# Row block 3 of h turned on chip for the w2 gradient, and the other h loads put into spent gradient slots, in a one-core forward-and-backward block

## The chip, the cores and the metric

The kernel runs on one core of one Trainium2 chip. A core has five engines that run side by side, each with its own instruction stream: TensorE (PE) multiplies matrices, VectorE (DVE) and ScalarE (ACT) work elementwise, GpSimd (POOL) does little here, and SyncE (SP) issues most of the DMA transfers; ACT and POOL issue some as well. The metric is the device time of the whole program in microseconds (us), the median of several executions.

## The reference

The reference runs a block forward and then the gradient of all its inputs for a given grad_out. It has 2048 rows (S) of width D = 512, and an MLP of hidden width F = 1792.

```python
mod = silu(c) @ w_mod -> sa, ca, ga, sb, cb, gb
h = layernorm(x) * (1 + ca) + sa
x = x + ga * irfft2(rfft2(h) * (w_r + 1j * w_i))
h = layernorm(x) * (1 + cb) + sb
r = relu(h @ w1 + b1);  h = r * r
x = x + gb * (h @ w2 + b2)
_out, _vjp = jax.vjp(_f, A_x, A_w_r, A_w_i, B_w1, B_b1, B_w2, B_b2, c, w_mod)
```

There are ten outputs: x, and nine gradients. Two matter below: the gradient of w1 (512 x 1792), a product of the MLP's input with the inner gradient, and the gradient of w2 (1792 x 512), a product of the hidden activation h = r² with the incoming gradient. Both sum over all 2048 rows.

## The kernel before

The rows are cut into NT = 16 tiles of 128, and four tiles make a row block (NB = 4 blocks). F is cut into NFC = 14 chunks of 128 ("fc"). The Fourier transforms are matrix products with constant tables. In order of time the stages are: start, layernorm 1, the first transform and `back_products` (L892: the gradient of h, kept in `gall` with 14 slots for each row block); the spectral forward stage; the MLP stage, block by block; the w1 gradient beside the spectral backward stage; and the w2 gradient beside the last row pairs of the spectral backward stage.

**MLP stage.** For each block, `stage_h` forms h for two fc at a time: four matmuls for each fc (L1064), ReLU on ACT, the square on DVE into a tile of the ring `hring`, and the product of r with the inner gradient in place in `gall` (L1071, ACT sums over it in L1073). Here h lies with f on the partitions and rows along them. `stage_o` multiplies h by w2, `stage_gn` the inner gradient by w1T (L1096, `row_product`). `hring` holds seven pairs, one block. For the w2 gradient, h is needed with rows on the partitions: each pair is stored in DRAM (`h_dram`, L1074), and is turned when it is read back. The inner gradient is turned from SBUF to SBUF, two fc of a block at a time (`ghn_part`, L1049, a DMA transpose of 128x8x128), and overwrites its slot in `gall`. `Cdb` and `LFb` (L1223, L1228) are tables, `h_sb` (L1234, four loads) is the other operand of the w1 gradient; it takes the place of w1T, so its loads wait for the last read of w1T in `stage_gn`.

**w1 gradient.** `grad_w1` runs 16 units (L1342): the first eight read the fc 0 to 6 of all blocks of `gall`, the last eight the fc 7 to 13.

**w2 gradient.** `grad_w2` (L1441) runs 14 groups, one for each fc, of 16 matmuls 128x512 over the 16 row tiles. Chunks 10 and 13 are cut in halves of 256 columns; the order is 0 to 9, 10a, 11, 12, 10b, 13a, 13b. ACT copies each result (L1442), and SP stores it (L1443; ACT itself the last half). `load_hn` (L1252) brings one fc of h from `h_dram`, turned, in one DMA transpose of 128x16x128 on SP's queue:

```python
pool = hnp if fc < 2 else endp.get("hn", endp["gw"])
hns.append(pool.tile([P, NT, P], BF16, name="hn", bufs=2 if pool is not endp.get("hn") else 6))
nc.sync.dma_start(hns[fc], h_dram[fc, :, :], transpose=True)
...
while len(hns) < min(NFC, max(fc + 4, min(2 * fc + 6, 10))):
```

So fc 0 and 1 have a pool that exists early, fc 2 and 3 another pair, fc 4 to 9 six buffers in the pool `endp`, which takes the place of `gall` once all units of the w1 gradient are done, and fc 10 to 13 reuse the buffers of fc 4 to 7. The tail's work tiles (gs, gh1, q1, gw) lie in the same pool.

**Row pairs.** Beside the w2 gradient, for t = 0, 2, ..., 14, `row_pair` and `row_end` finish two row tiles of the gradient of x on DVE and ACT. Each needs two loaded tiles (n1 and gxl, `load_rows3`, L1333 and L1334, on SP); the loads for t + 6 stand after the end of t. Then `gm.emit` (L488 to L502) forms a part of the gradient of w_mod with weights loaded in L481 (`wmc`), and L1563 to L1570 the gradient of c.

**What sets the order.** `set_order` arranges each engine's instructions by a table of numbers, ORDER, written out for PE, ACT, DVE, POOL and SP. An engine takes its stream strictly in that order, and so does SP with the transfers it issues: one that waits for a buffer, or takes long to issue, holds up all that stand behind it.

## Time and profile before

| | |
|---|---|
| median of 3 runs | 396.31 us (394.63, 396.31, 396.81) |
| span of the profiled execution | 398.0 us |
| PE busy | 382.1 us, 96% |
| DVE busy | 334.8 us, 84% |
| ACT busy | 303.2 us, 76% |
| MLP stage, about | 103 to 258 us |
| w1 gradient (L1342), about | 259 to 328 us |
| w2 gradient (L1441), about | 331 to 393 us |

The profile is of one execution, on the hardware. The span runs from its first to its last recorded event; it is the profiled execution's own time. A line of the timeline gives start and duration in us, the engine, the line of the code, the operation, "output<-input", a count, and in brackets the idle time before it and what ended that. SPq is SP issuing a transfer; its duration is the time for which SP is held by that issue, not the time of the transfer. "DMA to landing" is the time from the start of the issue to the arrival of the data. PEclk is the clock that TensorE was granted, 1.00 being full. Buffer names are those of the tiles, with a slot number (hn_1s is slot 1 of `hn`). "Waits" name an engine's instruction, what it waited for, the total time in us, the number of times and the longest.

### The profile page before, as it was taken

Reading aid. Unit: us, or ns where it says so; the run is one execution under the profiler, and the core shown is the slowest. Engines: PE = TensorE matmul, PEld = TensorE weight load, DVE = VectorE, ACT = ScalarE, POOL = GpSimd, SP = SyncE. Lnnn points to the kernel's source line nnn. Section 1 sums busy time; section 2 is a strip of 40 time slices with the busy share of each in tenths; the row PEclk is TensorE's granted clock in tenths of the full one; section 3 lists DMA queues with packets and bytes.
Section 4 is the critical chain, followed back from the end, with each engine's and each line's share of the span. In section 5 each row is a group of like instructions: output and inputs, shape, how many; then the busy total and the mean of one; then the engine's idle time right before and its main releaser. Section 6 shows DMA issues by size and latency. Waiting matters only on the chain.

```text
span 398.0 us, 8415 instructions
## 1 busy us (share of the span) xinstructions
PE 382.1 (96%) x3042; PEld 202.4 (51%) x3042; DVE 334.8 (84%) x822; ACT 303.2 (76%) x605; POOL 33.3 (8%) x114
## 2 busy tenths in 40 slices
PE   8999999999999999999999999999999999999495
PEld 3555677544444444444444435457666664444244
DVE  8899959949986699969997999957999989998430
ACT  4787899899896499759976999277665589998441
POOL 9151001000000000000000000012300000002100
PEclk9999999999999999999999999999999999999979
DMA  8999799874589999578928696999979998999995
GB/s 258 362 222 293 230 209 252 209 280 63 195 228 197 256 259 253 128 191 183 257 81 210 167 245 180 270 245 371 296 221 262 215 325 173 221 208 243 249 259 189
DMA packets 133957, 91.06 MB, mean 229 GB/s; under 512 B 86842, under 2 KB 119868, under 8 KB 133660
## 3 DMA queue, kind: packets, MB, share of 16 engines
q1 hardware_dynamic: 132904, 88.09, 87.1%
q0 software_dynamic: 832, 2.36, 1.8%
q8 instruction: 24, 0.39, 0.4%
q14 instruction: 17, 0.14, 0.1%
q10 hardware_dynamic: 180, 0.07, 0.1%
HBM read 38.70 MB, written 33.19 MB: 181 GB/s over the span
## 4 chain that ended last, share of the span: by engine, by line
PE 74%; ACT 12%; DMA 5%; DVE 4%; POOL 2%; issue 1%; SPq 0%; ACTq 0%; POOLq 0%; DVEq 0%
PE og_1s L1096 12%; PE og_0s L1096 11%; PE mm_0s L1441 6%; PE mm_1s L1441 6%; PE mm_0s L1342 5%; PE mm_1s L1342 5%; PE mm_1s L1064 4%; PE mm_0s L1064 4%; PE pst L1064 3%; DMA hn_1s<-h_dram 3%; PE mm_0s L892 2%; DMA Xb<-xs_dram 2%; ACT AE L359 2%; PE mm_1s L892 2%; ACT gab L896 2%; ACT gab L1073 1%
## 5 line engine op out<-in xcount | busy, mean ns | idle before, releaser
L1342 PEld LDWEIGHTS <-h_sb 128*64 128x64 bf16 (+1 forms) x464 | 28.7, 109 | 15.9 <-issue 0.9
L1073 ACT ACTIVATE gab<-gab 128x512 bf16<-128x512 bf16 x56 | 35.0, 648 | 0.5 <-DVE gab L1071 0.5
L1096 PEld LDWEIGHTS <-gab 128*128 128x128 bf16 x224 | 21.5, 98 | 27.0 <-ACT gab L1073 1.9
L1064 PEld LDWEIGHTS <-w 128*128 128x128 bf16 x224 | 21.2, 98 | 25.7 <-issue 1.7
L1342 PE MATMUL mm_0s<-gab,h_sb 128*64 128x384 bf16 (+2 forms) x288 | 32.7, 345 | 0.0
L892 PEld LDWEIGHTS <-w2T 128*128 128x128 bf16 (+1 forms) x280 | 22.9, 102 | 18.5 <-issue 3.9
L1096 PE MATMUL og_0s<-w1T,gab 128*128 128x512 bf16 x112 | 27.4, 379 | 0.2 <-ACT G_0s L1109 0.2
L1096 PE MATMUL og_1s<-w1T,gab 128*128 128x512 bf16 x112 | 27.6, 379 | 0.0
L1441 PE MATMUL mm_0s<-g_sb,hn_1s 128*128 128x512 bf16 x64 | 16.8, 423 | 6.0 <-DMA hn_1s<-h_dram 6.0
L1342 PE MATMUL mm_1s<-gab,h_sb 128*64 128x512 bf16 (+2 forms) x176 | 22.4, 370 | 0.0
L1064 PE MATMUL mm_1s<-h2T,w 128*128 128x512 bf16 x84 | 21.9, 379 | 0.0
L1064 PE MATMUL mm_0s<-h2T,w 128*128 128x512 bf16 x80 | 21.2, 379 | 0.0
L359 ACT ACTIVATE AE<-psB 128x1024 bf16<-128x1024 f32 x16 | 17.2, 1078 | 0.7 <-PE psB L355 0.6
L896 ACT CAST gab<-mm_1s 128x512 bf16<-128x512 f32 x24 | 14.8, 615 | 2.3 <-PE mm_1s L892 2.2
L892 PE MATMUL mm_0s<-gT_0s,w2T 128*64 128x512 bf16 (+1 forms) x76 | 16.1, 380 | 0.2 <-DVE gab L894 0.2
L892 PE MATMUL mm_1s<-gT_0s,w2T 128*128 128x512 bf16 (+1 forms) x72 | 15.6, 379 | 0.1
L1064 PE MATMUL pst<-h2T,w 128*128 128x512 bf16 x60 | 15.6, 379 | 0.0
L892 PE MATMUL mm_1s<-gT_1s,w2T 128*128 128x512 bf16 (+1 forms) x68 | 14.9, 379 | 0.3 <-ACT gab L896 0.2
L892 PE MATMUL mm_0s<-gT_1s,w2T 128*128 128x512 bf16 (+1 forms) x64 | 15.1, 379 | 0.0
L1441 PEld LDWEIGHTS <-hn_1s 128*128 128x128 bf16 x64 | 6.8, 107 | 15.3 <-DMA hn_1s<-h_dram 6.2
L321 POOL MEMSET AE<- 128x4 bf16 x4 | 0.4, 110 | 162.4 <-PE mm_1s L1064 162.4
L1441 PE MATMUL mm_1s<-g_sb,hn_0s 128*128 128x512 bf16 (+1 forms) x64 | 13.7, 352 | 0.0
(650 smaller groups left out, 1064.3 us busy)
## 6 DMA issues: line engine op xcount, KB each, us to landing
w<-in_B_w_dram SPq DMA_DIRECT2D x2, 1792.0 KB, 10.4
Xb<-xs_dram SPq DMA_DIRECT2D x4, 514.0 KB, 7.9
Z<-wz_dram SPq DMA_DIRECT2D x4, 514.0 KB, 7.5
x_sb<-in_A_x_dram SPq DMA_DIRECT2D x4, 512.0 KB, 6.2
n_dram<-x_sb SPq DMA_DIRECT2D x4, 512.0 KB, 6.2
h_dram<-h2r SPq DMA_DIRECT2D x8, 256.0 KB, 2.4
h_sb<-h_dram SPq DMA_DIRECT2D x4, 512.0 KB, 5.4
g_sb<-in_grad_out_dram SPq DMA_DIRECT2D x2, 1024.0 KB
```

The costliest lines, as they stand in the source:

```text
L321: nc.gpsimd.memset(ae[:, :, :, 256:257], 0.0)
L359: nc.scalar.activation(dst, ps.rearrange("p r b (e f) -> p (r b) f e", e=2), AF.Copy, scale=EF_S)
L892: nc.tensor.matmul(ps[m], lhsT=w2T[:, dc, fc * P + m.start:fc * P + m.stop], rhs=gT[b][:, :, dc, :], start=(dc == 0), stop=(dc == 3), **pos)
L896: nc.scalar.copy(out=gaT[b][:, fc, :], in_=ps)
L1064: nc.tensor.matmul(ps, lhsT=w1[:, dc, (fc + i) * P:(fc + i + 1) * P], rhs=h2T[b][:, :, dc, :], start=(dc == 0), stop=(dc == 3))
L1073: nc.scalar.activation(gh[:, i, :], gh[:, i, :], AF.Copy, accum_out=gb1[:, b, fc + i:fc + i + 1])
L1096: nc.tensor.matmul(ps, lhsT=lhs(fc), rhs=rhs[:, fc, :], start=(fc == 0), stop=(fc == NFC - 1))
L1342: nc.tensor.matmul(blocks(ps[m], fb), lhsT=h2_sb[:, t, dc * P + m.start:dc * P + m.stop], rhs=gh_rows(t, fb), start=(t == 0), stop=(t == N ...
L1441: nc.tensor.matmul(ps[:, 0:w], lhsT=hns[fc][:, t, :], rhs=g_sb[:, t, c:c + w], start=(t == 0), stop=(t == NT - 1))
```

## The change

1. The h tiles of row block 3 (the last) are not stored in `h_dram`, which shrinks to 12 row tiles. They stay in `hring`, and seven DMA transposes of 128x8x128 (L1243 of the new code) turn them from SBUF to SBUF into a new tile `hr`, on SP's queue during `stage_gn(3)`.
2. `load_hn` (L1287 of the new code) brings 12 row tiles, as 128x12x128, into spent slots of `gall`: fc goes to slots 14·(fc mod 4) + 3·(fc div 4 mod 2) and the two after it. That gives eight places, which are free once the first eight units of the w1 gradient have read them. Four loads stand at the point where two stood, four more where two more stood, and then one for each group; fc 8 to 13 reuse the places of fc 0 to 5. The group of fc reads `hr` for its last four row tiles (`h_rows`).
3. The tail's tiles gs, gh1, q1, gw come from `gall` as well (`place`, `Ring`), so `gall` is held to the end.
4. A pool `early` takes some tiles of `rows` (r, h2r, h2T, and n2rows of the even blocks). It is released before `Cdb` is loaded; that load now waits for the last reads and writes of these tiles.
5. ORDER is replaced for all five engines. The number of PE's rows is the same.

The diff, with most of the table cut:

```diff
...
     "SP": (
-        "3 1 0 2 4 6 5 8 7 38 24 9 20 22 12 25 27 29 28 21 26 30 55 10 23 11 13 33 31 36 32 35 34 37 14-15 39 16-18 40 47 44 41 "
...
+        "3 1 0 2 4 6 5 8 7 23 12 9 11 10 32 36 31 13 34 14 28-29 20-21 37 27 119 22 25 35 30 33 24 17 16 38 15 26 18 44 125 52 47 "
...
-    h_dram = dram.tile([NFC, P, NT * P], BF16, name="h_dram")
+    h_dram = dram.tile([NFC, P, (NT - TB) * P], BF16, name="h_dram")
...
+    early = Slots(tc, name="early", bufs=1)
...
-                    n2b[b] = rows.tile([P, TB, D], BF16, name="n2rows")
+                    n2b[b] = (rows if b % 2 else early).tile([P, TB, D], BF16, name="n2rows", bufs=1)
...
-                r = rows.tile([P, 2, SB], BF16, name="r")
+                r = early.tile([P, 2, SB], BF16, name="r", bufs=2)
...
-                nc.sync.dma_start(h_dram[fc:fc + 2, :, sl].rearrange("a p s -> p a s"), h2)
+                if b < NB - 1:
+                    nc.sync.dma_start(h_dram[fc:fc + 2, :, sl].rearrange("a p s -> p a s"), h2)
+                else:
+                    hpair[fc] = h2
...
+                early.release()
                 w1p.release()
                 cdp = Slots(tc, name="cdp", bufs=1, side="right")
                 K["Cd"] = cdp.tile([P, D], BF16, name="Cdb")
...
-                merge(stage_gn(b, UT), [x for p in zip(again, parts + [lambda: None]) for x in p])
+                hrp = Slots(tc, name="hrp", bufs=1, side="right")
+                hr = hrp.tile([P, NFC, TB, P], BF16, name="hr")
+                turns = [lambda fc=fc: nc.sync.dma_start(hr[:, fc:fc + 2].rearrange("p a j c -> p (a j) c"), hpair[fc].rearrange("p a s -> p (a s)"), transpose=True)
+                         for fc in range(0, NFC, 2)]
+                merge(stage_gn(b, UT), [x for p in zip(again, parts + [lambda: None], turns + [lambda: None]) for x in p])
...
+    spare = [NFC * b + 6 for b in range(NB)] + [NFC * b + k for b in range(NB) for k in range(7, NFC)] + [NB * NFC, NB * NFC + 1]
...
         if fc < NFC:
-            pool = hnp if fc < 2 else endp.get("hn", endp["gw"])
-            hns.append(pool.tile([P, NT, P], BF16, name="hn", bufs=2 if pool is not endp.get("hn") else 6))
+            a = NFC * (fc % 4) + 3 * (fc // 4 % 2)
+            hns.append(gall[:, a:a + 3, :].rearrange("p a (j c) -> p (a j) c", c=P))
             nc.sync.dma_start(hns[fc], h_dram[fc, :, :], transpose=True)
+
+    def h_rows(fc, t):
+        return hns[fc][:, t, :] if t < NT - TB else hr[:, fc, t - (NT - TB), :]
...
-                load_hn()
-                load_hn()
+                for _ in range(4):
+                    load_hn()
...
-                nc.tensor.matmul(ps[:, 0:w], lhsT=hns[fc][:, t, :], rhs=g_sb[:, t, c:c + w], start=(t == 0), stop=(t == NT - 1))
+                nc.tensor.matmul(ps[:, 0:w], lhsT=h_rows(fc, t), rhs=g_sb[:, t, c:c + w], start=(t == 0), stop=(t == NT - 1))
...
-        while len(hns) < min(NFC, max(fc + 4, min(2 * fc + 6, 10))):
+        while len(hns) < min(NFC, fc + 9):
             load_hn()
...
-    for _ in range(2):
+    for _ in range(4):
         load_hn()
...
-                    gap.release()
-                    endp["hn"] = endp["gm"] = Slots(tc, name="endp", bufs=2)
+                    endp["gs"], endp["gh1"], endp["q1"], endp["gw8"] = Ring(2, 6), Ring(2, 3), Ring(2, 3), Ring(1, 8)
...
-            gs = (endp["gm"].tile([P, 2, D], BF16, name="gs", bufs=6) if "gm" in endp and t >= 6 else fp.tile([P, 2, D], BF16, name="gs", bufs=3))
+            gs = (endp["gs"].tile() if "gs" in endp and t >= 6 else fp.tile([P, 2, D], BF16, name="gs", bufs=3))
...
```

**Place 1: SP's queue at the end of the MLP stage, before.** h_dram<-h are stores of h of block 3, gab<-gab the transposes of the inner gradient of blocks 2 and 3 (`gab` is the name of `gall`), gx_dram<-n2rows stores of row results.

```order
L1223 DMA Cdb<-Cd_dram 128x512
L1074 DMA h_dram<-h_4s 128x2x512
L1228 DMA LFb_3510<-LF_dram 128x1024
L1228 DMA LFb_3509<-LF_dram 128x1024
L1049 DMA_TRANSPOSE gab<-gab 128x8x128
L1074 DMA h_dram<-h_6s 128x2x512
L1074 DMA h_dram<-h_5s 128x2x512
L1049 DMA_TRANSPOSE gab<-gab 128x8x128 x2
L1134 DMA gx_dram<-n2rows_1s 128x1024
L1234 DMA h_sb<-h_dram 128x2048 x2
L1049 DMA_TRANSPOSE gab<-gab 128x8x128
L1234 DMA h_sb<-h_dram 128x2048 x2
```

The same place in the new program:

```order
L1235 DMA Cdb<-Cd_dram 128x512
L1243 DMA_TRANSPOSE hr<-h_2s 128x8x128
L1243 DMA_TRANSPOSE hr<-h_4s 128x8x128
L1243 DMA_TRANSPOSE hr<-h_1s 128x8x128
L1243 DMA_TRANSPOSE hr<-h_3s 128x8x128
L1243 DMA_TRANSPOSE hr<-h_5s 128x8x128
L1240 DMA LFb_3506<-LF_dram 128x1024
L1057 DMA_TRANSPOSE gab<-gab 128x8x128
L1250 DMA h_sb<-h_dram 128x2048
L1145 DMA gx_dram<-n2rows 128x1024
L1250 DMA h_sb<-h_dram 128x2048
L1057 DMA_TRANSPOSE gab<-gab 128x8x128
```

The stores of h are gone, and five of the seven new transposes stand between `Cdb` and the first load of `h_sb`. The other two follow the third load of `h_sb`, and one load of `h_sb` comes after them.

**Place 2: SP's queue at the start of the row pairs, before.** hn<-h_dram are reloads of h, n_0s and n_1s the n1 tiles of row pairs t = 0, 6, 12 and t = 2, 8, 14, out_dram<-Xb stores of another gradient.

```order
L1257 DMA_TRANSPOSE hn_5s<-h_dram 128x16x128
L1349 DMA out_dram<-gw_1s 128x896
L1402 DMA out_dram<-Xb 32x4x257
L1257 DMA_TRANSPOSE hn_0s<-h_dram 128x16x128
L1402 DMA out_dram<-Xb 32x4x257
L1257 DMA_TRANSPOSE hn_1s<-h_dram 128x16x128
L1334 DMA gxl_0s<-gx_dram 128x1024
L1333 DMA n_0s<-n_dram 128x1024
```

In the new program (n_5089 is the n1 tile of t = 4, the n_0s here that of t = 6, which waits for the end of row pair 0):

```order
L1287 DMA_TRANSPOSE gab<-h_dram 128x12x128
L1382 DMA out_dram<-gw_1s 128x896
L1367 DMA gxl<-gx_dram 128x1024
L1366 DMA n_0s<-n_dram 128x1024
L1366 DMA n_5089<-n_dram 128x1024
L1287 DMA_TRANSPOSE gab<-h_dram 128x12x128
L1432 DMA out_dram<-Xb 32x2x1028
L1367 DMA gxl_1s<-gx_dram 128x1024
```

These are the seventh and the eighth reload of the new program; in the old one hn_5s is the fourth. The n1 load of t = 4 stood 15 rows further up before; it now stands behind that of t = 6.

**Place 3: SP's queue in the last third of the w2 gradient, before.** out_dram<-gw are stores of finished groups.

```order
L481 DMA wmc_0s<-in_w_mod_dram 128x4x512
L1443 DMA out_dram<-gw_1s 128x512
L1257 DMA_TRANSPOSE hn_0s<-h_dram 128x16x128
L1334 DMA gxl_1s<-gx_dram 128x1024
L1257 DMA_TRANSPOSE hn_1s<-h_dram 128x16x128
L1443 DMA out_dram<-gw_2s 128x512
L1257 DMA_TRANSPOSE hn_2s<-h_dram 128x16x128
L481 DMA wmc_1s<-in_w_mod_dram 128x4x512
L1257 DMA_TRANSPOSE hn_3s<-h_dram 128x16x128
```

The last reloads of the new program:

```order
L481 DMA wmc_0s<-in_w_mod_dram 128x4x512
L1476 DMA out_dram<-gab 128x512 x3
L1287 DMA_TRANSPOSE gab<-h_dram 128x12x128 x2
L1367 DMA gxl_0s<-gx_dram 128x1024
L1476 DMA out_dram<-gab 128x512
L1367 DMA gxl_1s<-gx_dram 128x1024
```

Before, four reloads stand behind the store of the group that hn_0s waits on, and 18 stores come after the last of them. Now two reloads (fc 12 and 13) stand behind the stores of the first six groups, and both `wmc` loads are ahead of them. On PE, the transpose of `gcb` (L1567; L1599 in the new code) was the last instruction of all and now stands ahead of the last two half groups, 13a and 13b.

More of the change, by code (lines that the diff above doesn't have):

```diff
@@ L963 @@
         ghn = [None] * NB
+        hpair = {}
         late, late_f1 = Delayed(4), Delayed(4)
@@ L1015, in one @@
                 t = TB * b + j
-                h2r = rows.tile([P, 2, D], BF16, name="h2r", bufs=1)
+                h2r = early.tile([P, 2, D], BF16, name="h2r")
                 nc.vector.tensor_tensor(h2r, n2b[b][:, j:j + 2, :], modb[:, CB1_B, None, :].broadcast_to([P, 2, D]), op=ALU.mult)
@@ L1021, in one @@
                     if j == 0:
-                        h2T[b] = rows.tile([P, TB, 4, P], BF16, name="h2T", bufs=1)
+                        h2T[b] = early.tile([P, TB, 4, P], BF16, name="h2T")
                     K["h2T"] = nc.sync.dma_start(h2T[b][:, j:j + 2].rearrange("p j c q -> p (j c) q"), h2r.rearrange("p j d -> p (j d)"),
@@ L1030, in one @@
                 if j == 0:
-                    h2T[b] = rows.tile([P, TB, 4, P], BF16, name="h2T", bufs=1)
+                    h2T[b] = early.tile([P, TB, 4, P], BF16, name="h2T")
                 pst = psR.tile([P, D], FP32, name="pst2").bitcast(BF16).rearrange("p (c i q) -> p c i q", c=4, i=2)
@@ L1248, with place, __init__, tile @@
     gm = GMod(tc, K, scf, gsc, wm_view, out9_view)
-    hnp = Slots(tc, name="hnp", bufs=1, side="right")
     hns, endp = [], {}
+    spare = [NFC * b + 6 for b in range(NB)] + [NFC * b + k for b in range(NB) for k in range(7, NFC)] + [NB * NFC, NB * NFC + 1]
+    def place(n):
+        a = next(a for a in spare if all(a + k in spare for k in range(n)))
+        for k in range(n):
+            spare.remove(a + k)
+        return gall[:, a:a + n, :]
+    class Ring:
+        def __init__(self, n, k):
+            self.tiles, self.k = [place(n) for _ in range(k)], 0
+        def tile(self):
+            self.k += 1
+            return self.tiles[(self.k - 1) % len(self.tiles)]
     def load_hn():
@@ L1434, in grad_w2 @@
         if cols[0] == 0:
-            late_ = "gm" in endp
-            gwh[fc] = (endp["gm"] if late_ else gwp).tile([P, D], BF16, name="gw", bufs=8 if late_ else 2)
+            late_ = "gw8" in endp
+            gwh[fc] = endp["gw8"].tile()[:, 0, :] if late_ else gwp.tile([P, D], BF16, name="gw", bufs=2)
         gw = gwh[fc]
@@ L1505, in row_pair @@
             n1, gxl = rows3[t]
-            gh1, q1 = [(endp["gm"].tile([P, 2, D], BF16, name=x, bufs=3) if "gm" in endp and t >= 6 else fp.tile([P, 2, D], BF16, name=x, bufs=2)) for x in ("gh1", "q1")]
+            gh1, q1 = [(endp[x].tile() if "gs" in endp and t >= 6 else fp.tile([P, 2, D], BF16, name=x, bufs=2)) for x in ("gh1", "q1")]
             gn = fp.tile([P, 2, D], BF16, name="gn")
-            gs = (endp["gm"].tile([P, 2, D], BF16, name="gs", bufs=6) if "gm" in endp and t >= 6 else fp.tile([P, 2, D], BF16, name="gs", bufs=3))
+            gs = (endp["gs"].tile() if "gs" in endp and t >= 6 else fp.tile([P, 2, D], BF16, name="gs", bufs=3))
             rr = fp.tile([P, 2, 4], FP32, name="rr")
@@ L1576 @@
     lf2.release()
-    hnp.release()
     h2p.release()
+    hrp.release()
     cdp.release()
@@ L1582 @@
     endp["q"].release()
-    endp["gm"].release()
+    gap.release()
     set_order(tc)
```

170 rows, old and new, of the table ORDER are left out of this document.

## The prediction

> **What bounds the kernel now.** I read the page first (busy shares, then the chain), then TensorE's waits, then the timeline and windows around the one long wait, then SP's queue.
>
> ```profile
> PE 382.1 (96%) x3042; PEld 202.4 (51%) x3042; DVE 334.8 (84%) x822; ACT 303.2 (76%) x605; POOL 33.3 (8%) x114
> PEclk9999999999999999999999999999999999999979
> PE mm_0s L1441 <- DMA hn_1s<-h_dram: 6.0, 1, 6.0
> PE mm_0s L751 <- DVE ones_sq L83: 1.8, 1, 1.8
> PE psB L355 <- ACT AE L359: 0.8, 2, 0.7
> ```
>
> TensorE is busy for 96% of the span at full clock in nearly every slice, so the end is set by its stream and what interrupts it. It waits for long just once: 6.0 us in the w2 gradient, for a reload of h. The clock row dips in the slice behind that.
>
> ```profile
> 371.03 1.36 PE L1441 MATMUL mm_1s<-g_sb,hn_0s 128*128 128x256 bf16 x11
> 378.36 5.97 PE L1441 MATMUL mm_0s<-g_sb,hn_1s 128*128 128x512 bf16 x16 [5.96 <-DMA hn_1s<-h_dram]
> 384.16 3.62 PE L1441 MATMUL mm_1s<-g_sb,hn_2s 128*128 128x512 bf16 x16
> 378.40:381.40 3.00, 3.00 (x8) 1.07 (x9) 0.00 (x0) 0.96 (x3) 0.00 (x0) 0.50 1.18 264
> 381.40:384.30 2.90, 2.90 (x11) 1.17 (x10) 0.00 (x0) 2.48 (x5) 0.00 (x0) 0.70 1.15 224
> 384.30:388.00 3.70, 3.70 (x21) 1.76 (x19) 3.00 (x8) 0.77 (x2) 0.00 (x0) 1.00 0.99 271
> ```
>
> In the windows the columns are: stretch, us, busy us (count) of PE, PEld, DVE, ACT, POOL, then granted clock, DMA share, GB/s. The group of fc 11 takes 5.97 us after the wait, at a clock of 0.50 and then 0.70; the same 16 matmuls take 3.62 in the next group. The wait thus costs twice: itself, and 2.35 us (5.97 - 3.62) of slow clock.
>
> Why the reload is late is in SP's queue.
>
> ```profile
> 325.01 2.73 SPq L1257 DMA_TRANSPOSE hn_0s<-h_dram  x1
> 361.15 4.37 SPq L1257 DMA_TRANSPOSE hn_0s<-h_dram  x1
> 365.62 0.53 SPq L1334 DMA_DIRECT2D gxl_1s<-gx_dram  x1
> 366.24 5.22 SPq L1257 DMA_TRANSPOSE hn_1s<-h_dram  x1
> 372.41 7.57 SPq L1257 DMA_TRANSPOSE hn_2s<-h_dram  x1
> 380.70 3.94 SPq L1257 DMA_TRANSPOSE hn_3s<-h_dram  x1
> DMA to landing us min/median/max: 4.9/5.7/12.1
> ```
>
> Each reload holds SP for 2 to 8 us. Twelve of the fourteen are issued from 325.01 on, the last at 380.70; this one is issued right behind its neighbours, at 366.24, and lands at about 378.3, 12.1 us later, the longest of all.
>
> **Part 1: the reloads come earlier.** Two are issued before 325 now; in the new program eight places are free after half of the w1 units, and eight reloads stand ahead of row pair 0's end. The last two (fc 12, 13) stand behind the store of group 5. Groups take 3.6 us, so group 5 ends some 26 us before the end of the groups (6, 7, 8, 9, 10 in halves, 11, 12: seven lie between it and fc 13). A reload of 12.1 us from issue to landing, and a second behind a hold of up to 7.57, still make it. Each also carries 12 tiles instead of 16, three quarters of the bytes. So the wait goes: -6.0, and with it the slow clock: -2.35.
>
> The Trainium skill, "TensorE: Matmul & The Clock Gate", section on HAM oscillation, has a wait longer than the activity window of about 3.4 us put TensorE back to half clock until it has been busy for a window. The trace agrees that a wait of 5.96 us is followed by 0.50. By the page's one window the loss is an estimated 1.7 us (half of 3.4), 0.65 less than the row, and the sum would be 0.65 us smaller; I keep the row.
>
> **Part 2: the end.** The last group's copy ends at 393.47, ACT's store issue at 393.89, but SP is still issuing stores that the late reloads held back.
>
> ```profile
> 393.10 0.37 ACT L1442 CAST gw_5s<-mm_0s 128x256 bf16<-128x256 f32 x1 [1.38 <-PE mm_0s L1441]
> 393.50 0.39 ACTq L1443 DMA_DIRECT2D out_dram<-gw_5s  x1
> 395.26 0.29 SPq L1570 DMA_DIRECT2D out_dram<-gcr  x1
> span 398.0 us, 8415 instructions
> ```
>
> The end comes 2.45 us after SP's last issue (398.0 - 395.55). With no backlog it would come 2.45 after ACT's, at 396.3: up to -1.7. Fourteen store rows still follow SP's last reload rows, so I take half, -0.85. The other tail chain has room: DVE waits 10.8 us for the late `wmc`,
>
> ```profile
> DVE gm_junk L500 <- DMA wmc_1s<-in_w_mod_dram: 10.8, 1, 10.8
> ```
>
> and that load now stands ahead of the last reloads, so `gcb` comes up to 10.8 us earlier, while the half groups ahead of which its transpose now stands move up by 8.35 (6.0 + 2.35).
>
> **Part 3: turning block 3 on chip.** Seven transposes of 128x8x128 come onto SP's queue and seven stores go. The same shape from SBUF to SBUF is in the trace 28 times:
>
> ```profile
> L1049 SPq DMA_TRANSPOSE gab<-gab x28: 1231/1239/2031, 128.2 to 262.2; - x28
> 239.34 0.39 SPq L1074 DMA_DIRECT2D h_dram<-h_5s  x1
> L1071 DVE TENSOR_TENSOR gab<-r_1s,gab x14: 682/684/689, 108.7 to 235.5; 128x1024 bf16<-128x1024 bf16 x14
> L1096 PE MATMUL og_1s<-w1T,gab x112: 378/379/390, 130.3 to 245.6; 128*128 128x512 bf16 x112
> L1234 SPq DMA_DIRECT2D h_sb<-h_dram x4: 339/512/596, 246.0 to 248.8; - x4
> 259.18 0.62 PE L1342 MATMUL mm_0s<-gab,h_sb 128*64 128x512 bf16 x4
> 238.00:242.00 4.00, 3.79 (x30) 2.17 (x29) 3.96 (x12) 3.93 (x10) 0.00 (x0) 1.00 0.66 188
> 242.00:246.00 4.00, 4.00 (x26) 2.00 (x24) 3.46 (x10) 3.63 (x9) 0.00 (x0) 1.00 0.55 104
> ```
>
> Added hold 7 x 1.24 = 8.7 us, removed 7 x 0.39 = 2.7. What stands behind them is `h_sb`, which cannot start before w1T's last read at 245.6 anyway; block 3's h is complete at about 236 (L1071). Between lie 10 us, and five transposes hold 5 x 1.24 = 6.2. The other two, 2.5 us, and LFb stand ahead of the fourth load of `h_sb`: its issue goes from 248.8 to about 251.5 + 1.5 for what else shifts, 253, and with 5.4 us to landing (the median of L1234) it arrives at 258.4. The first unit starts at 259.18 and wants the last quarter of the rows about 2.7 us later, at 261.9. So the cost is 0, covered by 3.5 us. If each hold were the maximum, 2.03, five would hold 10.2 us and the last load would arrive about 2 us later still, before it is wanted. `Cdb` waits for the end of block 3's r now, and it is first used after 258: also 0. The DMA engines carry no more here: seven transposes replace seven stores of the same size, and share is 0.66 at 238 to 242.
>
> On these holds a page says otherwise: the Trainium skill, "DMA: Bandwidth & Descriptors", section "Issuing engines are not separate DMA queues", calls the time on the sequencer to initiate a DMA usually small relative to the DMA. The trace has 1.24 of 3.1 us for the small and 5.22 of 12.1 for the late one, not small. By the page the holds would cost nothing anywhere; by the page B below falls away, and its chance goes to the forecast.
>
> **Part 4: places, pool `early`, the new order.** The `gall` places need no new copy or instruction; PE has the same rows. The waits and the busiest stretch that bound the rest:
>
> ```profile
> PE psW_1s L796 <- ACT gT_0s L811: 0.4, 1, 0.4
> PE mm_0s L892 <- DVE gab L894: 0.2, 1, 0.2
> 270.37 0.70 DVE L444 TENSOR_TENSOR p<-Z,G_0s 128x1028 bf16<-128x1028 bf16 x1 [4.22 <-ACT G_0s L339]
> 331.00:366.00 35.00, 35.00 (x192) 16.00 (x193) 34.52 (x87) 32.18 (x68) 0.85 (x2) 1.00 1.03 216
> ```
>
> What the new order does to small waits is bounded from both sides: all other PE waits together are 3.8 us (the two shown above, 2.6, and five of 0.4 to 0.2), of which 1.8 lies at the start, so a gain ends at -3.8; for a loss the nearest row is a wait of DVE in the spectral backward stage, 4.2 us. The last line shows PE without a gap from 331 to 366, and DVE 34.52 busy of 35.00: PE has its w2 groups between the row pairs, DVE hardly any slack. I take +0.4, close to none, as the small waits of PE are mostly of that size or less.
>
> **Sum.** 398.0 - 6.0 - 2.35 - 0.85 + 0.4 = 389.2 for the profiled execution. That execution's span stands 1.69 above the median of 396.31; taking the same off gives **387.5 us** (2.2% less).
>
> **Rivals.**
>
> A, *a load of n1 waits and takes over part of the gain.* In the new order the n1 load of pair 4 stands behind that of pair 6, which waits for `row_end(0)`; the eighth reload stands behind both.
>
> ```profile
> 333.11 1.58 ACT L1528 ACTIVATE gn_0s<-n_0s,rr_0s 128x512 bf16<-128x512 bf16 x2
> 335.80 0.68 DVE L1517 TENSOR_TENSOR q_0s<-gh_0s,n 128x1024 bf16<-128x1024 bf16 x1
> DMA to landing us min/median/max: 3.2/4.2/8.9
> ```
>
> `row_end(0)` reads its n1 until 334.7; two issues take some 0.9, the landing 4.2 in the median (L1333), so n1 of pair 4 comes at 339.8 where DVE reads it at 335.8: up to 4.0 us on a DVE that has no slack. If that passes to PE's end in full, 387.5 + 4.0 = 391.5. Against it: PE has groups of w2 to run meanwhile.
>
> B, *slower: the new transposes hold SP as the reloads do.* If the 128x8x128 of `hr` held not 1.24 but 3.94 us (as L1257 at 380.70), five would hold 19.7: from 236.2 to 255.9, and the first `h_sb` load would start there, the fourth 255.9 + 3 x 0.5 + 2 x 3.94 + 2 = 267.2, landing 5.4 later at 272.6. It is wanted at 261.9: PE stands for 10.7 us in the middle of the first unit, with the slow clock after it, 2.35. 387.5 + 10.7 + 2.35 = 400.5. It decides from a hold of about 2.5 us on. For it: holds grow where the DMA engines are full (7.57 at a share of 1.16). Against it: the 28 of the same kind never passed 2.03, and the share there was 0.55 to 0.66.
>
> C, *the change does not do what it says: the late reload is no earlier, or the wait returns.* The DMA engines are full from 331 to 384 (share 1.03 to 1.18), so an early issue may still land late; a reload that misses by what is left, or a new order that loses what the bound of 4.2 allows twice over, gives back nearly all: 387.5 + 8.4 = 395.9. Against it: seven groups, 25 us, lie between the last reloads' turn and their use.
>
> **How the numbers follow.** Forecast 0.72, A 0.12, C 0.08, B 0.08. The range: below, the rest of the drain (0.85) and most of the small waits after the start (2.0) gives 384.6, and a little for the runs' own spread (394.63 is 1.7 under its median), 384.0; above, A with the spread on top, 391.5 + 1.7, and a little of the order's loss, 393.5. That leaves out B and C, 0.16. 0.5%, 2 us here, is about what a measurement of this kernel can tell from no change. The forecast and A are faster (0.84), C lies within it (0.08), B is slower (0.08).
>
> **What would show each step.** Right: no wait of PE on a reload of 1 us or more in the w2 gradient; clock 1.00 through the last 30 us; the group of fc 11 at about 3.6 us; eight reloads issued before 335; SP's last issue within 1 us of ACT's last. The seven transposes (L1243) at 1.2 to 2.0 us each, the first unit of the w1 gradient at about 259 without a gap in it. Wrong: a wait of PE on `h_sb` of several us (B), of DVE on n1 at pair 4 (A), or on any reload (C); a w1 gradient that starts later than 260 would mean that the new order lost time before it, which no term here has.

## The result, and the profile after

The changed kernel takes 405.98 us in the median of 4 runs (405.24 to 406.11), the kernel before 395.47 beside it (394.44 to 396.81): a ratio of 1.0273 [1.0232, 1.0314]. It is 2.7% slower, where 2.2% faster was forecast. Times here are medians of all executions; each ratio leaves out, on both sides, executions more than 1.5% above the fastest of the same kernel. Its profiled execution took 406.01 us with a span of 404.2. So the time lies 1.8 above the span, and the first profile of before, with 398.0, was of an execution of about 399.8 us, some 4 above that kernel's median. A second one was profiled for that reason (the first experiment); its stages are set beside the new ones here.

From the page of the changed kernel:

```profile
span 404.2 us, 8374 instructions
PE 386.2 (96%) x3013; PEld 205.2 (51%) x3042; DVE 338.0 (84%) x822; ACT 305.8 (76%) x605; POOL 34.8 (9%) x114
PEclk9999999999999999999999999999999999999999
```

TensorE's longest waits:

```profile
PE psT L401 <- ACT utcs L391: 1.2, 1, 1.2
PE mm_0s L757 <- DVE ones_sq L83: 1.1, 1, 1.1
PE psG_0s L385 <- DVE utcs L389: 1.0, 2, 0.8
PE acc L1531 <- DVE gab L1549: 0.9, 1, 0.9
```

By this list the change did what was asked of it: no wait for a reload is left, and the clock row dips nowhere. Yet the kernel is later. The end does not say where; the points that both programs pass do. Ends of stages on TensorE, in us (span of before in its second profile 392.1):

| TensorE | before, first profile | before, second | after | after minus second |
|---|---|---|---|---|
| first transform ends | 48.6 | 48.4 | 52.8 | 4.4 |
| first matmul of the MLP stage's h | 102.8 | 102.5 | 108.3 | 5.8 |
| last matmul of block 3's h | 232.1 | 231.8 | 240.2 | 8.4 |
| last of gn and o | 258.3 | 258.0 | 267.2 | 9.2 |
| w1 gradient ends | 328.1 | 327.1 | 340.8 | 13.7 |
| last matmul of the w2 gradient | 393.1 | 388.4 | 400.9 | 12.5 |
| span | 398.0 | 392.1 | 404.2 | 12.1 |

Eight of the twelve us are gone before a single row of h is turned, 4.4 of them in the first 53. The matmuls of h, in the view of one line (instructions, ns of one, first and last start), of the second profile of before and of after:

```profile
L1064 PE MATMUL pst<-h2T,w x60: 379/379/389, 102.5 to 229.3; 128*128 128x512 bf16 x60
```

```profile
L1072 PE MATMUL pst<-h2T,w x60: 376/379/379, 108.3 to 236.9; 128*128 128x512 bf16 x60
```

A matmul costs the same; the stream is late. The start shows how, in the window of the first 12 us of before (first profile) and of after, with the columns as in the prediction:

```profile
0.00:12.00 12.00, 10.09 (x58) 4.45 (x59) 10.06 (x68) 5.60 (x10) 10.60 (x63) 1.00 0.85 279
```

```profile
0.00:12.00 12.00, 9.76 (x22) 2.56 (x23) 4.64 (x35) 4.12 (x7) 6.63 (x48) 1.00 0.84 277
```

DVE does 35 instructions where it did 68, PE 22 matmuls where it did 58. DVE's timeline in after, with the idle time before an instruction in brackets:

```profile
5.53 0.69 DVE L825 BATCH_NORM_STATS2 l_st_2s<-x_sb 128x6 f32<-128x512 bf16 x1 [1.35 <-DMA x_sb<-in_A_x_dram]
8.06 0.34 DVE L149 TENSOR_SCALAR gen_v_0s<-cd_fr,cd_d 128x256 int32<-128x256 int32 x1
11.83 0.23 DVE L130 COPY TAT<-sm_ps 128x128 bf16<-128x128 bf16 x1 [3.43 <-PE sm_ps L128]
```

The new table puts the first statistics of x, which wait for a load, and the copy of TAT, which waits for a transpose on PE, ahead of work of DVE that needs neither. An engine takes its rows strictly in order, so that work (tables, which PE needs next) stands too. PE's busy time of 9.76 us hides that its matmuls run slow. L757 (L751 before) issues 30 matmuls of a constant tile, whose result nothing reads. Half of them in the view of the line, of before (first profile) and of after:

```profile
L751 PE MATMUL mm_0s<-ones_sq x15: 376/379/634, 1.8 to 12.3; 128*128 128x512 bf16 x15
```

```profile
L757 PE MATMUL mm_0s<-ones_sq x15: 377/584/631, 1.1 to 16.6; 128*128 128x512 bf16 x15
```

In before they take 0.63 us each at first and 0.38 from 5.9 us on in the second profile, from 7.7 in the first; in after they take 0.63 until about 11.4, and the transpose of TAT, at 11.48, stands behind 17 of them where it stood behind 14. The clock row reads 1.00 all the while. After has a gap of 0.67 us on PE at 2.7 us, a wait for `ident` of POOL, which before does not have there; whether that gap keeps the matmuls slow was not tried.

A second loss lies in the w1 gradient (its stretch in the second profile of before, and in after):

```profile
258.90:327.10 68.20, 67.91 (x925) 44.44 (x923) 59.30 (x133) 45.58 (x82) 6.93 (x18) 1.00 0.98 279
```

```profile
267.60:340.80 73.20, 69.54 (x919) 47.85 (x923) 60.47 (x131) 45.61 (x80) 9.46 (x21) 1.00 0.99 260
```

As many weight loads, 923, take 73.20 us for 68.20. PE is idle for 3.66 of them (73.20 - 69.54) where it was idle for 0.29, in waits of 0.2 to 0.8 us, and its busy time holds the other 1.6. It is not quite the same work: eight more sums into `acc` (L966, 16 for 8 before) and a few other matmuls have moved into the stretch, and five of L401 out of it. So the 5.0 us are not all loss. Over both stages, from the first matmul of the w1 gradient to the last of the w2 gradient, after takes 133.3 us (400.9 - 267.6), the two profiles of before 133.9 and 129.5, each with a late reload in it.

SP's queue at the end of the MLP stage, in after:

```profile
241.74 1.24 SPq L1057 DMA_TRANSPOSE gab<-gab  x1
243.46 0.32 SPq L1235 DMA_DIRECT2D Cdb<-Cd_dram  x1
243.83 1.24 SPq L1243 DMA_TRANSPOSE hr<-h_2s  x1
249.31 1.34 SPq L1243 DMA_TRANSPOSE hr<-h_5s  x1
```

And the views of the lines of `h_sb` and of the reloads (instructions, ns of one as minimum, median and maximum, first and last start):

```profile
L1250 SPq DMA_DIRECT2D h_sb<-h_dram x4: 325/426/581, 253.3 to 262.5; - x4
```

```profile
L1287 SPq DMA_TRANSPOSE gab<-h_dram x14: 1398/2295/4900, 311.6 to 382.8; - x14
```

The five transposes take from 243.83 to 250.65, 6.8 us for the 6.2 forecast. A reload of 12 tiles holds SP for 1.4 to 4.9 us; one of 16 held it for up to 7.57.

The end, ACT's last instructions and SP's last issue:

```profile
400.93 0.37 ACT L1475 CAST gab<-mm_0s 128x256 bf16<-128x256 f32 x1 [1.26 <-PE mm_0s L1474]
401.34 0.38 ACTq L1476 DMA_DIRECT2D out_dram<-gab  x1
401.46 0.28 SPq L1348 DMA_DIRECT2D out_dram<-b4r_0s  x1
```

From the last copy's end (401.30) to the end of the span it is 2.9 us, where it was 4.5 (398.0 - 393.47).

### The profile page after: what moved, and what is told of

Read it like the earlier page. It is cut to its first block, busy times and chain, and to the rows that moved or that the text cites. A ratio compares the mean times of both kernels' runs of the same rounds, so it can differ in the third digit from the quotient of the medians.

```text
span 404.2 us, 8374 instructions
## 1 busy us (share of the span) xinstructions
PE 386.2 (96%) x3013; PEld 205.2 (51%) x3042; DVE 338.0 (84%) x822; ACT 305.8 (76%) x605; POOL 34.8 (9%) x114
## 5 line engine op out<-in xcount | busy, mean ns | idle before, releaser
L1375 PEld LDWEIGHTS <-h_sb 128*64 128x64 bf16 (+1 forms) x464 | 31.9, 109 | 13.4 <-issue 0.2
L1107 PEld LDWEIGHTS <-gab 128*128 128x128 bf16 x224 | 21.2, 98 | 25.9 <-ACT gab L1081 1.9
L1474 PEld LDWEIGHTS <-gab 128*128 128x128 bf16 x192 | 18.3, 98 | 18.3 <-issue 2.4
L1107 PE MATMUL og_0s<-w1T,gab 128*128 128x512 bf16 x108 | 26.1, 379 | 0.4 <-ACT gab L1081 0.3
L1107 PE MATMUL og_1s<-w1T,gab 128*128 128x512 bf16 x109 | 26.1, 379 | 0.2
L1072 PE MATMUL mm_1s<-h2T,w 128*128 128x512 bf16 x84 | 23.2, 379 | 0.3 <-issue 0.2
L1474 PE MATMUL mm_1s<-g_sb,gab 128*128 128x512 bf16 (+1 forms) x94 | 20.2, 352 | 0.5 <-ACT gab L1475 0.4
L1474 PE MATMUL mm_0s<-g_sb,gab 128*128 128x512 bf16 (+1 forms) x92 | 19.7, 351 | 0.2
L359 ACT ACTIVATE AE<-psB 128x1024 bf16<-128x1024 f32 x16 | 16.6, 1038 | 3.2 <-PE psB L355 1.9
L1072 PE MATMUL pst<-h2T,w 128*128 128x512 bf16 x60 | 16.7, 379 | 0.4 <-ACT r_1s L1073 0.3
L898 PE MATMUL mm_1s<-gT_1s,w2T 128*128 128x512 bf16 (+1 forms) x68 | 15.8, 378 | 0.1
L401 PEld LDWEIGHTS <-utcs 128*128 128x128 bf16 x128 | 9.9, 97 | 11.1 <-issue 2.6
```

Source lines behind the costliest of these rows:

```text
L359: nc.scalar.activation(dst, ps.rearrange("p r b (e f) -> p (r b) f e", e=2), AF.Copy, scale=EF_S)
L401: nc.tensor.matmul(ps[:, P * i:P * i + P], lhsT=CS[:, i, t].rearrange("p a b -> p (a b)"), rhs=K["Cf"][:, i, :], start=True, stop=True)
L898: nc.tensor.matmul(ps[m], lhsT=w2T[:, dc, fc * P + m.start:fc * P + m.stop], rhs=gT[b][:, :, dc, :], start=(dc == 0), stop=(dc == 3), **pos)
L1072: nc.tensor.matmul(ps, lhsT=w1[:, dc, (fc + i) * P:(fc + i + 1) * P], rhs=h2T[b][:, :, dc, :], start=(dc == 0), stop=(dc == 3))
L1107: nc.tensor.matmul(ps, lhsT=lhs(fc), rhs=rhs[:, fc, :], start=(fc == 0), stop=(fc == NFC - 1))
L1375: nc.tensor.matmul(blocks(ps[m], fb), lhsT=h2_sb[:, t, dc * P + m.start:dc * P + m.stop], rhs=gh_rows(t, fb), start=(t == 0), stop=(t == N ...
```

## The experiments

The first theory was that the new order loses the time, from the start on; the rival, that the edit's code does: its transposes, places and the pool `early`. A third point was the base: that the wait of 6.0 us belongs to one execution. All ratios are to the kernel before, run beside each kernel.

**e0, the kernel before, profiled again.** No edit.

> The kernel before, unchanged, for a second profile of it. The first profile has a span of 398.0 us and a wait of 6.0 us for a reload, while its runs have a median of 395.5 and device times lie about 1.8 above their span (406.0 against 404.2 in the new kernel), so that profile is of a long execution. Theory S (the wait is partly of that one execution): a span of about 394, a wait of PE on hn_1s of 0 to 3 us. Rival (the wait is there in every execution and something else varies): a wait of 5 to 6.5 us.

The run took 394.26 us, with a span of 392.1. Its wait for a reload and the group behind it:

```profile
PE mm_1s L1441 <- DMA hn_2s<-h_dram: 2.9, 1, 2.9
378.04 5.16 PE L1441 MATMUL mm_1s<-g_sb,hn_2s 128*128 128x512 bf16 x16 [2.92 <-DMA hn_2s<-h_dram]
377.00:380.00 3.00, 1.96 (x5) 0.74 (x6) 0.00 (x0) 0.00 (x0) 0.00 (x0) 0.63 1.17 273
380.00:383.00 3.00, 3.00 (x12) 1.23 (x11) 2.58 (x7) 0.59 (x1) 0.00 (x0) 0.80 1.09 305
```

It is another reload, it waits for half as long, and the group behind it loses 1.54 us (5.16 - 3.62) for 2.35. The price of the late reload was 4.5 us here and 8.3 in the first profile; that accounts for 3.8 of the 5.9 us between their spans. The Trainium skill, "TensorE: Matmul & The Clock Gate", section on HAM oscillation, puts the danger at gaps above about 3.4 us. This trace does not agree: with a gap of 2.92 the clock fell, to 0.63 in the mean from 377 to 380 and to 0.80 in the next 3 us.

**e1, the new code with the old order.** All engines in the old order; on SP the new rows have to stand somewhere (here and in the next experiments the fences give SP's rows around `Cdb` by their outputs; hr are the seven transposes):

```diff
 Cdb
+hr x5
 LFb x2
 gab x3
 h_sb x2, gab, h_sb
+hr x2
 h_sb
```

The stores of block 3's h go out of the queue, and the reloads move up to where their places come free.

> The new program's code with the old table of the order: PE, ACT, DVE and POOL exactly as in the kernel before (these four engines have the same instructions in both), SP in the old order with the block 3 stores left out, the seven on-chip transposes where the new table has them (five behind Cdb, two behind the third h_sb load), and the reloads moved up to the first places that are free. Theory O (the new table costs the time, the edit itself gains what was forecast): 386 to 392 us. Rival E (the edit costs it: transposes on SP, the pool early, places in gall): 402 us or more. In between, both have a part.

403.53 us, 1.0218 [1.0113, 1.0323], in the range of rival E. Up to the end of gn and o (258.0) its stages agree with those of before to 0.1 us; the new code costs nothing there:

```profile
L1063 PE MATMUL pst<-h2T,w x60: 379/379/389, 102.5 to 229.3; 128*128 128x512 bf16 x60
```

Behind that it stalls, in a place of its own:

```profile
PE mm_0s L1366 <- DMA h_sb<-h_dram: 7.5, 2, 6.3
SPq L1226 <- DVE h_5s L1066: 7.0, 1, 7.0
258.00:265.00 7.00, 0.99 (x17) 0.39 (x13) 4.08 (x8) 1.07 (x2) 0.00 (x0) 0.73 1.05 278
265.00:272.00 7.00, 5.47 (x28) 2.03 (x28) 0.00 (x0) 1.07 (x2) 1.31 (x5) 0.50 1.01 254
```

SP stands for 7.0 us at `Cdb`, which now waits for DVE's last work on block 3's h, and the five transposes behind it hold SP for 6.8 more; everything queued behind it is late, down to `h_sb`, and PE stands 7.5 us for the w1 gradient, with the slow clock after it. That the code loses time later in this order doesn't yet say that it does in the new one.

**e2, the old code with the new order.** Nothing of the new code but its tables. The seven stores that only the old code has are put back on SP between the transposes of the inner gradient, the last two of them between `Cdb` and `h_sb`.

```diff
-ORDER = OLD
+ORDER = NEW
```

> The code of the kernel before with the new table of the order for PE, ACT, DVE and POOL, and on SP the new order with the seven stores of block 3 put back behind transposes of the inner gradient, and the reloads where their old buffers come free (the first two early, the others after the w1 gradient). Theory O: as slow as the new kernel, 403 to 410 us. Rival E: 394 to 398 us, as before.

423.42 us, 1.0696 [1.0602, 1.0789], outside what either theory gave. The reloads come far too late in this mixture (waits of 5.7, 2.6 and 2.4 us), so the total says nothing. What stands is the part before any reload: the first transform ends at 51.7, h starts at 107.0 and block 3's ends at 238.7, where after has 52.8, 108.3 and 240.2 and before 48.4, 102.5 and 231.8:

```profile
L1067 PE MATMUL pst<-h2T,w x60: 376/379/379, 107.0 to 235.4; 128*128 128x512 bf16 x60
```

So the table alone, without the new code, makes about 7 of the 8.4 us up to there.

**e3, e9 and e5, the new kernel with part of the old order.** Every engine first takes the instructions that before had started by a given time, in the old order; the rest follows in the new one:

```diff
-ORDER[e] = NEW[e]
+P = [i for i in OLD[e] if start_before[e][i] < T]
+ORDER[e] = P + [i for i in NEW[e] if i not in P]
```

with T = 16, 50.3 and 200 us. The first, e3 (50.3 us):

> The new kernel, but what the kernel before had started by 50.3 us (the start, layernorm 1, the first transform) is run first and in the old order, on all five engines; the rest follows in the new order. Nothing of the edit lies in this stretch. In the profiles the new kernel is 4.2 us late at its end. Theory O: that is the table's and stays to the end, so 401 to 402.5 us. Rival (later waits swallow it, the loss is made further on): 405 to 406.5 us.

401.89 us, 1.0134 [1.0064, 1.0203]: 4.1 us below the changed kernel. e9 (16 us):

> The new kernel, but what the kernel before had started by 16 us runs first and in the old order; the rest in the new one. With the old order up to 50.3 us it was 401.9 (-4.1). In the profile the first matmul of back_products is 3.2 us late (17.9 against 14.7), with a wait of DVE of 3.4 us for the transpose that PE does at 11.5 in place of 7.9. Theory: the loss of the start is made in these first us: 402 to 403.2. Rival: it is made later in layernorm and the first transform: 405 or more.

401.83 us, 1.0165 [1.0096, 1.0234]: the same 4.1 us. All that e3 gained is lost in the first 16 us, where DVE stands and PE's matmuls run slow; in e9's profile they take 0.38 us from 6.4 on. In e2, the other program with the whole new table, they do so from 9.2. e5 (200 us):

> The new kernel, but everything that the kernel before had started by 200 us (up to the third row block of the MLP stage) runs first and in the old order on all five engines; the rest in the new order. Nothing of the edit but the pool early lies in that stretch. The new kernel's profile is 7 to 8 us late there, and the run with the old start alone gave 401.9 (4.1 less than 406.0). Theory O (the table costs the time there): 398 to 399.5 us. Rival E (the pool early or the rest costs it): 401 to 402.5, no better than the old start alone.

397.09 us, 1.0048 [1.001, 1.0085], 8.9 below the changed kernel: another 4.8 us (3.4 by the ratios, since the kernel before differed beside the two) come from the order between 50 and 200 us. With them 8.9 of the 10.5 us are back, and the code is all new. What is left, 1.6 us (1.9 by the ratio), and the gain that was forecast and does not appear, lie behind 200 us; whether in the code or in the order there, this run does not tell. Its profiled execution took 406.19 us; of e5 only the times are used.

**e6, e1 with `h_sb` ahead.**

```diff
 hr x5
+h_sb x4
 LFb x2
 gab x3
-h_sb x2
 gab
-h_sb
 hr x2
-h_sb
```

> The new code in the old order as in the run before (403.5 us), with one change on SP: the four loads of h_sb stand right behind the first five on-chip transposes, ahead of two table loads and three transposes of the inner gradient; the last two on-chip transposes stand later. That run waited 7.5 us for h_sb, at a clock of 0.72 to 0.74 for some 26 us, and its w1 gradient ended at 339.8 in place of 327.1. Theory Q (SP's queue ahead of h_sb is the whole price of the edit there): no wait on h_sb, the w1 gradient starts at 259, 388 to 393 us. Rival D (seven more transposes and the early reloads cost DMA time in the w1 gradient, wherever they stand): the wait goes but the w1 gradient stays long, 396 to 400 us.

405.14 us, 1.0273 [1.0156, 1.0389]: the wait for `h_sb` is gone, the w1 gradient starts at 258.9, and it takes 82.6 us for 68.2. Neither theory had that. New waits stand in it:

```profile
PE mm_1s L488 <- POOL sel L1287: 7.1, 1, 7.1
PE mm_1s L1321 <- DVE b L1319: 3.7, 1, 3.7
269.64 0.52 POOL L1285 MEMSET sel<- 128x512 bf16 x1 [30.16 <-DMA hr<-h_6s]
```

`sel`, a small table, lies in the memory that block 3's h gives up, so it waits for the last of the seven transposes; `b` is late behind it. Moving one row up in SP's queue moved another down, and another reader was behind it.

**e7, e6 with the reloads where before had them.**

```diff
-ORDER["SP"] = E6
+ORDER["SP"] = [E6 with its reload rows at the positions of the reload rows in OLD]
```

> As the run with h_sb first, but the fourteen reloads stand where the kernel before has them (two early, twelve from the row pairs on) in place of the first free places. They still are of 12 tiles, and go into the same places. Theory R (early reloads are the gain at the end): 3 to 5 us slower than the run with h_sb first, with a wait of PE on a reload. Rival (smaller reloads alone do it): the same within 1 us, no wait.

404.06 us, 1.0245 [1.015, 1.034], and no wait for a reload: the early position, on which the prediction built, is not what takes the wait away. The last reload is issued 16.3 us ahead of the last matmul (382.4, 398.7), where the second profile of before has 16.6. Reloads of 12 tiles into free places are enough at the old positions too, in a program whose w1 gradient ends 15 us late.

**e8, e1 with the transposes spread.**

```diff
-gab, Cdb, hr x5, LFb x2, gab x3, h_sb x2, gab, h_sb, hr x2, h_sb, gab
+gab x2, Cdb, hr, gab, hr, LFb x2, gab, hr, h_sb x2, hr, gab, h_sb x2, hr x2, gab, hr
```

> The new code in the old order, with SP's queue at the end of the MLP stage arranged anew: the first transpose of block 3's inner gradient ahead of Cdb, then the seven on-chip transposes of h one by one between the transposes of the inner gradient, which wait for each other about 3 us each anyway; h_sb in two pairs as in the kernel before; reloads where the kernel before has them. In the two runs with the five transposes in a row, Cdb was issued 6.9 us later than before (it waits for the pool early) and the five held SP for 6.9 more, so the inner gradient's transposes came up to 14 us late, and POOL's sel, which lies in the place of the ring of h, waited for the last on-chip transpose. Theory Q (SP's queue there, Cdb's wait and the row of transposes, is the whole price): the w1 gradient lasts 68 to 72 us from 259, 391 to 395 us in all. Rival D (seven more transposes cost DMA time wherever they stand): 399 us or more.

399.54 us, 1.0097 [1.0056, 1.0139], in the range of rival D, though less than half of e1's loss is left. `sel` still comes late,

```profile
265.18 0.52 POOL L1285 MEMSET sel<- 128x512 bf16 x1 [25.69 <-DMA hr<-h_6s]
```

and the w1 gradient takes 75.9 us.

**e11, all seven transposes ahead of the first two `h_sb` loads.**

Against e8:

```diff
-gab x2, Cdb, hr, gab, hr, LFb x2, gab, hr, h_sb x2, hr, gab, h_sb x2, hr x2, gab, hr
+gab x2, Cdb, hr x2, gab, hr x2, LFb x2, gab, hr x3, h_sb x2, gab, h_sb x2, gab
```

> As the run with the on-chip transposes between those of the inner gradient (399.5 us, w1 gradient 75.9 us long, sel at 265.2 after the last on-chip transpose), but all seven now stand ahead of the first h_sb pair. Theory Q (what was left of the price is sel and b, which wait for the ring of h to be turned): sel at 258 to 259, the w1 gradient 68 to 71 us, 392 to 395 us. Rival D (the seven transposes delay the inner gradient's own transposes and the loads that follow, wherever they stand): 398 us or more.

399.13 us, 1.0012 [0.997, 1.0054]: no difference from before by the ratio, but its ten runs go from 395.25 to 405.39, and their median lies in the range of rival D (before beside them: 396.68, from 392.3 to 401.78). Its profiled execution took 403.25 us. There `sel` comes at 258, as theory Q had it, and PE waits for `h_sb` in its place, whose first load is issued at 253.8 (245.8 in the second profile of before):

```profile
258.09 0.52 POOL L1285 MEMSET sel<- 128x512 bf16 x1 [18.57 <-PE og_1s L1098]
PE mm_0s L1366 <- DMA h_sb<-h_dram: 4.1, 1, 4.1
```

So the new code in the old order costs from little to 2.7%, by where SP's rows stand, and in none of these orders does it gain. That the transposes also cost time as DMA work is not ruled out.

**e12, before with only the pool `early`.** The old order, no transpose on chip, no new place:

```diff
+early = Slots(tc, name="early", bufs=1)
-n2b[b] = rows.tile([P, TB, D], BF16, name="n2rows")
+n2b[b] = (rows if b % 2 else early).tile([P, TB, D], BF16, name="n2rows", bufs=1)
...
-r = rows.tile([P, 2, SB], BF16, name="r")
+r = early.tile([P, 2, SB], BF16, name="r", bufs=2)
...
+early.release()
 w1p.release()
```

> The kernel before with the pool early alone: r, h2r, h2T and n2rows of the even blocks lie in it, and it is given back before Cdb is loaded. The old order and everything else unchanged. In the runs with the new code in the old order Cdb was issued at 239.2 in place of 232.3, since it waits for the last use of early by block 3's stage_h. Theory C (that wait is a part of the price at the start of the w1 gradient, because SP stands at Cdb and the inner gradient's transposes come behind it): Cdb at 238 to 240, the first of those transposes some 5 us later, the w1 gradient 2 to 5 us longer, 398 to 402 us. Rival (the transposes of h are the whole price): Cdb late, but the w1 gradient as before, 395 to 397 us.

403.7 us, 1.0191 [1.0118, 1.0263], 1.7 us above the range of theory C; the rows are as it had them. SP's wait, and its rows around it:

```profile
SPq L1225 <- DVE h_5s L1068: 6.8, 1, 6.8
230.86 1.40 SPq L1050 DMA_TRANSPOSE gab<-gab  x1
239.19 0.34 SPq L1225 DMA_DIRECT2D Cdb<-Cd_dram  x1
241.05 1.23 SPq L1050 DMA_TRANSPOSE gab<-gab  x1
```

In the second profile of before the same three rows are

```profile
230.97 1.23 SPq L1049 DMA_TRANSPOSE gab<-gab  x1
232.30 0.54 SPq L1223 DMA_DIRECT2D Cdb<-Cd_dram  x1
235.09 1.23 SPq L1049 DMA_TRANSPOSE gab<-gab  x1
```

`Cdb` itself is in nobody's way; it is read after 258. The transpose behind it comes 6 us later, and those of the inner gradient follow one another, each into the place that the one before has read. The w1 gradient takes 73.0 us for 68.2.

**e13, e12 with `Cdb` and the LFb loads behind the `h_sb` loads.**

```diff
-Cdb
-LFb x2
 gab
 ...
 h_sb x2
+Cdb
+LFb x2
```

> The kernel before with the pool early (403.7 us), but the loads of Cdb and of the two tables LFb stand behind the four h_sb loads on SP, so that nothing that is due earlier waits behind Cdb's wait for the pool. Theory H (the price of the pool early is SP standing 6.8 us at Cdb, with the transposes of the inner gradient behind it): those transposes at 235 to 247 as in the kernel before, the w1 gradient 68 to 69 us long, 394.5 to 397.5 us. Rival L (Cdb, the tables or what else lies in that place come too late themselves): 400 us or more, with a wait of PE on LFb or Cdb.

397.35 us, 1.0084 [1.0039, 1.013]: with `Cdb` behind the urgent rows the pool costs 0.8% for 1.9%. The two intervals overlap a little (1.0118 to 1.013), the medians are 6 us apart, and the w1 gradient takes 69.9 us for e12's 73.0. The transpose behind the old place of `Cdb` is back at its time, and `Cdb` issues without holding it:

```profile
235.27 1.24 SPq L1047 DMA_TRANSPOSE gab<-gab  x1
249.34 0.46 SPq L1222 DMA_DIRECT2D Cdb<-Cd_dram  x1
```

**e10, before with only the places in `gall`.** Old order but for the reloads, 16 tiles each, no transpose on chip:

```diff
-pool = hnp if fc < 2 else endp.get("hn", endp["gw"])
-hns.append(pool.tile([P, NT, P], BF16, name="hn", bufs=2 if pool is not endp.get("hn") else 6))
+if fc % 7 < 3:
+    hns.append(hnp.tile([P, NT, P], BF16, name="hn", bufs=3))
+else:
+    a = NFC * (fc % 7 - 3)
+    hns.append(gall[:, a:a + 4, :].rearrange("p a (j c) -> p (a j) c", c=P))
...
-endp["hn"] = endp["gm"] = Slots(tc, name="endp", bufs=2)
+endp["gs"], endp["gh1"], endp["q1"], endp["gw8"] = Ring(2, 6), Ring(2, 3), Ring(2, 3), Ring(1, 8)
```

> The kernel before with the second and third part of the change alone: all of h goes through DRAM as before, in 16 tiles, nothing is turned on chip, no pool early, no hr. The reloads get seven places that are free early: three in their own pool (it has the room that hr would take) and four in the slots of gall that the first eight units of the w1 gradient have read; the tail's tiles lie in the rest of gall. The old order on all engines, SP with the reloads moved up by about two rows of the queue, seven ahead of the first group in place of four. In the kernel before the wait for a reload was 6.0 us in one profile and 2.9 in the other, and its runs spread from 392.6 to 402.7. Theory P (the late reload is the wait, and earlier places remove it without a price): 390 to 393 us, no wait of PE on a reload, runs within 2 us of each other. Rival (DMA time, not the places, makes the last reloads late): a wait of 2 us or more on a reload, 394 to 397.

400.81 us, 1.0079 [1.0024, 1.0133]; both expectations were wrong. No wait for a reload is left, and others took its place:

```profile
PE mm_1s L1456 <- ACT gab L1457: 4.5, 1, 4.5
PE psT_1s L401 <- ACT Tsb_3s L403: 4.3, 1, 4.3
ACT gab L1457 <- DMA out_dram<-gab: 7.2, 1, 7.2
DVE gab L1545 <- DMA gxl_1s<-gx_dram: 7.5, 1, 7.5
```

From the w1 gradient's end to the last matmul it takes 68.8 us, where the two profiles of before have 65.0 and 61.3. SP's reloads now come early, and the stores and row loads behind them late: ACT waits 7.2 us for a store to free its tile, PE 4.5 for ACT; at the start of that stretch PE waits 4.3 for ACT, which waits for another store.

## Why the prediction was wrong, point by point

**The order (part 4) is the step that failed.** It was given +0.4, with -3.8 and +4.2 as bounds drawn from the waits in the trace of before. Up to block 3's h it costs 8.4 us in the profiles, and putting the old order back up to 200 us returns 8.9 of the 10.5 (e5); the old order in the first 16 us alone returns 4.1 (e9), and the new table in the old code loses 6.9 up to the same point (e2). The bounds were of the wrong kind: the waits that an order has did not bound those of another order. The rows of the new order would have shown a part: on DVE the copy of TAT stands ahead of rows that build tables (L225, L231 and the second L149), and its transpose on PE behind 17 matmuls of L757. That these would run at 0.63 us until 11.4, no row shows. The prediction read SP's rows at three places and no row of DVE or PE before 100 us. Its own last sentence, that a w1 gradient starting later than 260 means an order that lost time earlier, is what the trace showed: 267.6.

**`Cdb` at 0 (part 3) left a cost out.** The wait was seen, its reader was looked for and found late, and the cost was called 0. What stands behind it on SP was not priced. Alone, the pool costs 1.9% (e12), and over half of that goes when `Cdb` stands behind its neighbours (0.8%, e13). In the changed kernel the order partly answers that: `Cdb` issues at 243.46, 1.7 us after the row ahead of it. What it costs there was not measured.

**The transposes and `h_sb` (part 3) were right in the changed kernel.** The five ahead of `h_sb` hold SP for 1.24 to 1.40 us each, the last two for 2.49 and 2.06 (the forecast's most was 2.03), and PE has no wait for `h_sb`: its last load is issued at 262.5, which is 253.3 with the 9.2 us of delay taken off, and 253 was forecast. In the old order PE has a wait of 7.5 us (e1), the stall that rival B put at 10.7, but by SP standing at `Cdb` and five holds of the usual length, not by long ones. Missed was a reader at the other end: what lies in the memory that h gives up (`sel`, 7.1 us in e6).

**The reload's wait (part 1) went, for another reason and for less.** It is gone; in e7 it is gone with the reloads at their old places in the queue too, so their size and the free places suffice there; no run parts these two. Of the eight reloads forecast to be issued before 335, five were; the eighth came at 348.2, in a program whose w1 gradient ends 13.7 us late. Worth 8.35 us in the first profile, it is worth 4.5 in the second, which ran near the median. The sum took 8.35 from an execution that stood some 4 us above the median, and then took a distance to the median off as well, 1.69, which set a span (398.0) against times (396.31); what made that execution long was largely the wait itself, so a part of it was counted twice. From the second profile the same terms give 394.26 - 4.5 - 0.85 + 0.4 = 389.3. From the w1 gradient's end to the last matmul after takes 60.1 us: 4.9 less than the first profile of before, 1.2 less than the second. But the w1 gradient ahead of it takes 5.0 us more, so over both stages nothing is gained on the second profile (133.3 for 129.5). Where that gain went stays open. e10, with like places and 16 tiles, shows one way: no wait for a reload, and waits for ACT behind SP's early reloads in its place.

**The end (part 2) was right:** 1.6 us less, of a forecast 0.85 and up to 1.7. **Rival A** did not come at pair 4: DVE has no wait for that n1. It has one of 2.6 us for the n1 of a late pair, at 378, with 0.9 of PE behind it:

```profile
DVE gab L1549 <- DMA n_1s<-n_dram: 2.6, 1, 2.6
```

**Rival C**, that the bound of 4.2 is passed twice over, comes nearest in size (8.4), but had the loss beside a returned wait and ended level; here the order's loss stands against a gain that on the median execution was half as large.

**Open.** The stretch of the w1 gradient takes 5.0 us more in the changed kernel, a part of it work that moved in. e12 has nearly the same with the pool alone (73.0); no run separates pool and table there. Why the first matmuls run slow for longer wasn't tried, nor which engine's rows make the loss between 50 and 200 us, nor what is left of e13's 0.8%. No version ran faster than the kernel before.

## What to carry to other kernels

When a change replaces a written order, price the order as a change of its own: read each engine's rows from the first one on for an instruction that waits ahead of one that is ready, and compare the stages' ends before looking at the stage that was edited. A list of waits does not show matmuls that run slow; their times do. When a transfer on an in-order queue gets a new wait, its price is that of all that stands behind it, not of its own reader. Price a wait only when a second profile of the same kernel confirms it.

## What the runs showed of the hardware

The kernel before is not one time: its runs beside the experiments went from 392.3 to 402.7 us, and in one set of eleven (beside e13) the span went from 390.7 at a mean clock of 0.998 to 399.8 at 0.985. The changed kernel's four runs lie within 0.9 us at a clock of 1.00. That the late reload, landing differently each time, makes that spread fits the two profiles, but is not shown: the twelve runs of e10, whose profile has no wait for a reload, go from 395.73 to 404.77 too.

At the start the clock row reads 1.00 while a 128x512 matmul takes 0.63 us, and 0.38 later: from 7.7 and 5.9 us on in the two profiles of before, from 9.2 in e2 and from 12.0 in after.

A gap of 2.92 us on TensorE was enough for the clock to fall, to means of 0.63 and 0.80 in the two windows of 3 us around and behind it (e0); the group of matmuls there took 5.16 us for 3.62. After one of 6.3 us it was still 0.50 from 265 to 272 (e1), with short gaps in between.
